# Seven partial products in two more pairs of the first layer, and the sums that they need made beside attention's last units

## Chip, cores and metric

One core of a Trainium2 chip runs the whole kernel. The metric is the device time of one execution in microseconds (us), as the median of several executions. TensorE (PE) multiplies; VectorE (DVE), ScalarE (ACT) and GpSimd (POOL) do the element work; SyncE (SP) issues the loads.

## What is computed

Clustered attention, then two feed-forward layers, all in float32:

```python
mask = q_assign[:, :, :, None] == k_assign[:, :, None, :]
scores = np.where(mask, scale * q @ k.T, -1e9)     # 2 x 8 heads, 768 x 768, head_dim 64
x = softmax(scores) @ v                            # as 1536 tokens x 512
h = x @ w_in;  x = np.maximum(0.01 * h, h) @ w_out # layer one: 512 -> 2048 -> 512
h = x @ w_in2; out = np.maximum(h, 0) ** 2 @ w_out2
```

The assignments are the nearest of 16 centroids, for queries and keys apart; `scale` is 1/8.

## The kernel before

**Precision.** Every float32 operand is kept as two parts, high and low (`xh`/`xl`, `wh`/`wl`, `gh`/`gl`, `th`/`tl`), and every product is three matmuls: high by high, high by low, low by high. A high part is a rounding copy, mostly on ACT; a low part is a subtraction, on POOL or DVE.

**Attention.** 48 units of 256 query rows are taken through scores (`S`), softmax (`e`), transposes (`T`), the split of the transposed weights (`eh`, `el`) and the product with v (`A`). ACT copies one half of `A` out and DVE adds the other (`fold_a`, `fold_b`, into `xt`). When a pair of heads is complete, `xsplit` makes its 128 columns of `xh` and `xl`. The eighth pair of heads holds the last 128 columns for the second 768 tokens.

**The layers.** Tokens are three blocks of 512 (0, 1, 2). The 2048 hidden columns are 16 blocks of 128, taken two at a time: a *pair*, named by its first block (f = 0, 2, ... 14). A weight block is loaded by SP as raw 8-byte words into the one buffer `wraw` (1 MB); ACT (`mag`), POOL (`low`) and DVE (`join`) make float32 words `wt` of it, and only then may the next load start; ACT makes `wh` and POOL `wl`. These steps are the pieces 1 to 4 of `decode_pieces`.

**Plain and seven.** In a plain pair the token blocks are multiplied one by one (`g1`: hidden units `h`; `g2`: outputs `o`). In a pair of the list `SEVEN`, tokens 0 and 1 and the two halves of a weight form 2 x 2 blocks, and seven products take the place of eight, in the first step (`P1` to `P7`) and the second (`M1` to `M7`). This needs sums of weight blocks (`sum_pieces`: four quarter-size operations on POOL into `ws`, then `wh` on ACT and `wl` on POOL) and sums of x: `t1` to `t4`, for both 128-column parts kk = 0 and 1 of each half, each made of whole blocks (`w11`, `w12`, `w21`, `w22`: high plus low, on DVE) by subtraction, and then split into `th` (ACT) and `tl`. `P1`'s result is copied out (`k1`, on ACT) before `P6` is added to the same PSUM bank.

Before, layer one has pairs f = 0 and 2 plain. Pair f = 4 has a plain first step and a seven-product second step (`SEVEN_PLAIN`). The pairs f = 6 to 14 use seven products in both steps.

**Order.** Each engine runs its own instructions in program order and waits on semaphores. From the end of attention to pair f = 2 a scheduler merges the recorded pieces; elsewhere (`manual_schedule`) the engines keep the written order: `PLAN`, `RAMP` and the `SEVEN_...` strings, where each word is one step (`n` the next pair's weights, `u` token block 2, `B` and `T` activations and their sums, `r`, `f`, `o` the flushes).

Of the kernel before, what the change touches and what calls it, by code (L numbers as in the profile page):

```python
# [15 lines left out]
ALU = mybir.AluOpType  # L16
# [47 lines left out]
)  # L64
SEVEN_REST = (
# [34 lines left out]
def attention_moe_moe_kernel(  # L100
# [178 lines left out]

    vp = ast.enter_context(tc.tile_pool(name="vp", bufs=2))  # L280
# [3 lines left out]
    xtp = ast.enter_context(tc.tile_pool(name="xtp", bufs=2))  # L284
# [269 lines left out]
    T_t = {}  # L554

# [58 lines left out]
    def fold_b(u):  # L614
        p, j = divmod(u // UPH, 2)
        c = (u % UPH) * 256
        x = xt_t[p][64 * j : 64 * j + 64, c : c + 256]
        et_t.pop(u)
        nc.vector.tensor_tensor(out=x, in0=a_t.pop(u)[64 * j : 64 * j + 64], in1=x, op=ALU.add)  # L619

    def xsplit(p, part):
        b, hp = divmod(p, HP)
        sl = slice(b * S, (b + 1) * S)
        if part == 0:
            pool_copy(out=xh[:, hp, sl], in_=xt_t[p])
        else:
            nc.gpsimd.tensor_tensor(
                out=xl[:, hp, sl], in0=xt_t.pop(p), in1=xh[:, hp, sl].bitcast(F32), op=ALU.subtract
            )
# [249 lines left out]
    for u in range(-1, NU + 5):  # L879
        if u == NU - UPP:  # L880
            pst.close()
            stg.append(ctx.enter_context(tc.tile_pool(name="stg", bufs=1, side="right", reuse_waits="tile")))
            wpx = ctx.enter_context(tc.tile_pool(name="wpx", bufs=SIDE, side="right", reuse_waits="tile"))
            ring.append((wpx, SIDE))
        if u == NU - 2:
            manual.close()
        for op in PLAN[u % UPP].split():
            if ":" in op:
                name, lag = op.split(":")
                i = u - int(lag)  # L890
# [20 lines left out]
    gp = ctx.enter_context(tc.tile_pool(name="gp", bufs=6, reuse_waits="tile"))  # L911
# [38 lines left out]
    def g1(m, b, f):  # L950
# [5 lines left out]
        return h  # L956

# [96 lines left out]
    def seven(m, f, prev, after, later):  # L1054
# [35 lines left out]
        for name, n, b, block in (  # L1090
            ("g00", "V", 0, f0), ("g01", "U", 0, f1), ("g10", "W", 1, f0), ("g11", "X", 1, f1)
        ):
            ops[name] = lambda n=n, b=b, block=block: prod(
                n, [w_in(block, k) for k in ks], [x_in(k, b) for k in ks], True
            )
# [51 lines left out]
        def unit(j):  # L1147
            st[f"u{j}"] = bank(1 + j * m)
# [108 lines left out]
        for kk in range(2):  # L1257
# [4 lines left out]
            (0, 4): SEVEN_PLAIN, (0, NF - 2): SEVEN_LAST, (1, 2): SEVEN_SEAM, (1, NF - 2): SEVEN_END  # L1262
# [4 lines left out]
    def t_ops(m, kk):  # L1267

        st = {}

        def whole(out, k, b):
            if m:
                st[out] = acc[:, b, k]
                return
            h, l = x_in(k, b)
            st[out] = tmp()
            nc.vector.tensor_tensor(
                out=st[out], in0=h.bitcast(F32), in1=l.bitcast(F32), op=ALU.add
            )

        def minus(out, x, y, *tag):
            st[out] = tmp(*tag)
            nc.gpsimd.tensor_tensor(out=st[out], in0=st[x], in1=st[y], op=ALU.subtract)

        def high(i, t):
            nc.scalar.copy(out=th[:, i, kk], in_=st[t])

        def low(i, t):
            nc.gpsimd.tensor_tensor(
                out=tl[:, i, kk], in0=st[t], in1=th[:, i, kk].bitcast(F32), op=ALU.subtract  # L1290
            )

        def t4():
            minus("t4", "b21", "t2", "t4", 2)
            t_late[kk] = st["t4"]

        def t1():
            if m:
                whole("b12", kk, 1)
                whole("b11", kk, 0)  # L1300
                whole("b22", 2 + kk, 1)
                whole("b21", 2 + kk, 0)
            minus("t1", "b12", "b11")

        return {
            "w12": lambda: whole("b12", kk, 1),
            "w11": lambda: whole("b11", kk, 0),
            "w22": lambda: whole("b22", 2 + kk, 1),
            "w21": lambda: whole("b21", 2 + kk, 0),
            "t1": t1,  # L1310
            "t2": lambda: minus("t2", "b22", "t1"),
            "t3": lambda: minus("t3", "b22", "b12"),
            "t4": t4,
            "h1": lambda: high(0, "t1"),
            "h2": lambda: high(1, "t2"),
            "h3": lambda: high(2, "t3"),
            "l1": lambda: low(0, "t1"),
            "l2": lambda: low(1, "t2"),
            "l3": lambda: low(2, "t3"),
            "h4": lambda: t_last(kk),  # L1320
        }

    def t_last(kk):
        h, l = x_in(kk, 1)
        t = t_late.pop(kk)
        nc.scalar.copy(out=h, in_=t)
        nc.vector.tensor_tensor(out=l, in0=t, in1=h.bitcast(F32), op=ALU.subtract)

    t_late = {}

    def step_list(m, f, prev):
# [28 lines left out]
        else:  # L1360
# [5 lines left out]
        ((0, 1),), ((0, 2),), ((1, 0),), ((0, 3),), ((0, 4), (1, 1)),  # L1366
        ((1, 2),), ((2, 0),), ((1, 3), (1, 4), (3, 0)), ((2, 1),), ((2, 2),),
# [31 lines left out]
    t_by = [[t_ops(m, kk) for kk in range(2)] for m in range(2)]  # L1399

    def sums(m, turn):
        for op in SUMS[m].get(turn, "").split():
            name, kk = op.split(".")
            t_by[m][int(kk)][name]()

    prev = []
    for m in range(2):
        turn = 0
        for f in range(0, NF, 2):
            if (m, f) == (0, 2):  # L1410
                order.enter_context(
                    tc.manual_schedule(
                        engines={
                            mybir.EngineType.PE,
                            mybir.EngineType.DVE,
                            mybir.EngineType.Activation,
                            mybir.EngineType.Pool,
                        }
                    )
                )  # L1420
# [71 lines left out]
```

## Time and profile before

| | |
|---|---|
| median of 3 runs | 738.1 us (737.52 to 738.11) |
| the profiled execution | 737.28 us |
| its span, first to last instruction | 735.6 us |
| PE busy | 729.3 us (99%) |
| POOL / DVE / ACT busy | 580.0 / 555.2 / 491.3 us |
| chain that ended last, share on PE | 94% |
| granted TensorE clock | 1.0 of full speed in every slice |

The span is cut by the profile into busy and idle time for each engine; 1.7 us of the execution's 737.28 lie outside it. Attention ends near 250 us, layer one near 485, layer two at the end.

### The profile page before, as it was taken

To read this page: it belongs to the slowest core of one execution; us is meant where nothing else is said; L and a number is where in the kernel's file an instruction comes from. 1 tells how busy PE (TensorE), PEld (TensorE's weight loads), DVE (VectorE), ACT (ScalarE), POOL (GpSimd) and SP (SyncE) were. 2 spreads that over 40 slices of the span, in tenths; PEclk is the share of its full clock that TensorE was granted. 3 is DMA by queue.
4 is the path that set the end of the run, shared out by engine and by line. 5 is a ranking of instruction groups with operands and counts; after the bars stand their busy time and mean duration, and the time that the engine had idled before them with its cause. 6 is when DMAs were issued, how large, how long until landed. Compare 5 with 4: busy or idle time off the path is not lost.

```text
span 735.6 us, 11900 instructions
## 1 busy us (share of the span) xinstructions
PE 729.3 (99%) x4264; PEld 647.3 (88%) x4264; DVE 555.2 (75%) x879; ACT 491.3 (67%) x909; POOL 580.0 (79%) x534
## 2 busy tenths in 40 slices
PE   9999999999999999999999999999999999999998
PEld 8999999999998888888888888888888898888987
DVE  7999999999998535476766867787676685866847
ACT  7988988988998464456364473657748457484561
POOL 7999999999957648766787877899798786777841
PEclk9999999999999999999999999999999999999999
DMA  5694574572602311111131121211113112121004
GB/s 150 168 224 111 108 186 111 113 180 68 160 22 95 121 70 60 57 58 57 59 115 57 58 91 54 85 57 58 58 58 115 57 58 61 60 110 57 1 1 172
DMA packets 17755, 65.57 MB, mean 89 GB/s; under 512 B 3120, under 2 KB 6320, under 8 KB 12704
## 3 DMA queue, kind: packets, MB, share of 16 engines
q1 hardware_dynamic: 17696, 64.81, 30.0%
q8 instruction: 34, 0.56, 0.3%
q14 instruction: 25, 0.20, 0.1%
HBM read 43.02 MB, written 3.15 MB: 63 GB/s over the span
## 4 chain that ended last, share of the span: by engine, by line
PE 94%; ACT 2%; DVE 2%; POOL 1%; issue 1%; POOLq 0%; ACTq 0%; DVEq 0%
PE h L933 33%; PE o L1170 17%; PE h L1170 10%; PE A L597 8%; PE S L500 8%; PE T L562 7%; PE o L1011 7%; PE S L370 1%; ACT e L532 1%; DVE nm L522 1%; PE warm L310 1%; DVE el L579 1%; ACT eh L573 0%; PE dots L370 0%; POOL e L549 0%
## 5 line engine op out<-in xcount | busy, mean ns | idle before, releaser
L933 PE MATMUL h<-xl,wh 128*128 128x512 f32 x288 | 112.3, 390 | 0.0
L933 PE MATMUL h<-xh,wl 128*128 128x512 f32 x288 | 112.2, 390 | 0.0
L933 PE MATMUL h<-xh,wh 128*128 128x512 f32 x288 | 112.2, 391 | 0.0
L1124 POOL TENSOR_TENSOR gl<-t,gh 128x512 fp32r<-128x512 f32 x52 | 73.1, 1426 | 36.4 <-ACT gh L1121 26.5
L579 DVE TENSOR_TENSOR el<-T,eh 128x512 fp32r<-128x512 f32 x144 | 94.6, 683 | 2.9 <-ACT eh L573 2.2
L549 POOL TENSOR_SCALAR e<-e,r 128x768 f32<-128x768 f32 x96 | 86.3, 908 | 12.7 <-PE T L562 6.8
L532 ACT ACTIVATE e<-S,nm 128x768 f32<-128x768 f32 x96 | 87.3, 909 | 9.8 <-DVE ds L398 5.3
L522 DVE TENSOR_REDUCE nm<-S 128x1 f32<-128x768 f32 x96 | 90.9, 948 | 3.6 <-PE S L370 1.9
L187 POOL TENSOR_TENSOR wl<-ws,wh 128x1024 fp32r<-128x1024 f32 x25 | 60.5, 2419 | 41.8 <-ACT wh L186 41.8
L500 PE MATMUL S<-hb 128*128 128x384 f32 (+1 forms) x384 | 89.5, 347 | 0.1
L187 POOL TENSOR_TENSOR wl<-wt,wh 128x1024 fp32r<-128x1024 f32 x31 | 76.0, 2451 | 12.9 <-ACT wh L186 12.2
L573 ACT CAST eh<-T 128x512 fp32r<-128x512 f32 x144 | 79.7, 590 | 8.8 <-PE T L562 8.6
L597 PE MATMUL A<-eh,vv 128*128 128x256 f32 x288 | 80.3, 308 | 0.6 <-DVE xt L619 0.6
L562 PE MATMUL T<-ident,e 128*128 128x128 f32 x576 | 79.7, 273 | 0.5 <-POOL e L549 0.5
L597 PE MATMUL A<-el,vv 128*128 128x256 f32 x288 | 73.0, 283 | 0.2 <-DVE el L579 0.2
L562 PEld LDWEIGHTS T<-ident,e 128*128 128x128 f32 x576 | 68.9, 143 | 3.6 <-POOL e L549 0.7
L212 ACT ACTIVATE wt<-wraw 128x1024 f32<-128x1024 f32 (+1 forms) x33 | 36.7, 1111 | 49.6 <-POOL ws L267 46.3
L1063 DVE TENSOR_TENSOR h<-h,q 128x512 f32<-128x512 f32 x36 | 25.2, 699 | 54.2 <-PE h L933 48.6
L933 PEld LDWEIGHTS h<-xh,wh 128*128 128x128 f32 x288 | 54.1, 188 | 12.0 <-DVE gl L1124 0.9
L933 PEld LDWEIGHTS h<-xh,wl 128*128 128x128 f32 x288 | 54.0, 188 | 11.3
L500 PEld LDWEIGHTS S<-hb 128*128 128x128 f32 (+1 forms) x384 | 62.2, 189 | 1.6 <-ACT e L532 1.4
L933 PEld LDWEIGHTS h<-xl,wh 128*128 128x128 f32 x288 | 54.1, 188 | 10.6
(190 smaller groups left out, 2051.0 us busy)
## 6 DMA issues: line engine op xcount, KB each, us to landing
wraw<-w SPq DMA_DIRECT2D x32, 1024.0 KB, 4.7
hb<-spl SPq DMA_DIRECT2D x14, 576.0 KB, 4.7
hb<-spl SPq DMA_DIRECT2D x42, 192.0 KB, 5.1
rqk<-qk SPq DMA_DIRECT2D x16, 384.0 KB, 3.7
rv<-v SPq DMA_DIRECT2D x8, 384.0 KB, 3.3
out<-q SPq DMA_DIRECT2D x11, 256.0 KB, 2.2
hb<-st SPq DMA_DIRECT2D x56, 24.0 KB, 1.9
hb<-hb SPq DMA_DIRECT2D x5, 144.0 KB, 8.1
```

The lines of the kernel that those rows point to most:

```text
L187: return lambda eng=nc.gpsimd: eng.tensor_tensor(out=wl, in0=t, in1=wh.bitcast(F32), op=ALU.subtract)
L500: nc.tensor.matmul(out=s[:, c, 0:HALF], lhsT=hb[0:k, a, i * 128 : (i + 1) * 128], rhs=hb[0:k, b, c * HALF : (c + 1) * HALF], start=(a == 0 ...
L522: nc.vector.tensor_reduce(out=n, in_=s_t[t][:, :, 0:HALF], axis=AX.XY, op=ALU.max, negate=True)
L532: nc.scalar.activation(out=e.rearrange("p (a b) -> p a b", a=2), in_=s_t.pop(t)[:, :, 0:HALF], func=AF.Exp, bias=n_t.pop(t), scale=1.0, ac ...
L549: nc.gpsimd.tensor_scalar(out=e_t[t], in0=e_t[t], scalar1=r_t[t // 2][:, t % 2 : t % 2 + 1], scalar2=1.0, op0=ALU.mult, op1=ALU.mult,)
L562: nc.tensor.transpose(T[:, o : o + 128], e_t[2 * u + b][:, kc * 128 : (kc + 1) * 128], ident)
L573: nc.scalar.copy(out=eh[:, 2 * g : 2 * g + 2, :].rearrange("p a b -> p (a b)"), in_=T_t[u, g])
L579: nc.vector.tensor_tensor(out=el[:, 2 * g : 2 * g + 2, :].rearrange("p a b -> p (a b)"), in0=T_t.pop((u, g)), in1=eh[:, 2 * g : 2 * g + 2, ...
L597: nc.tensor.matmul(out=A, lhsT=w, rhs=m[:, kc, :], start=(kc == 0 and i == 0), stop=(kc == KC - 1 and i == 1),)
L933: nc.tensor.matmul(out=out, lhsT=l, rhs=r, start=(first and i == 0), stop=(i == n - 1), skip_group_check=not first,)
L1124: eng.tensor_tensor(out=lo[n], in0=full[n], in1=hi[n].bitcast(F32), op=ALU.subtract)
L1170: nc.tensor.matmul(out=out, lhsT=l, rhs=r, start=(fresh and i == 0), stop=(stop and i == 2), skip_group_check=True,)
```

## The change

- Pairs f = 2 and f = 4 of layer one now use seven products in both steps; f = 2 follows a new order, `SEVEN_TOP`. Three more weight-sum blocks are made.
- The sums of x no longer have two plain pairs in which to be made. Part of them is recorded beside attention's units 46 and 47 (`EARLY_SUMS`), the rest in pair f = 0. They are subtracted in place. Four of the `tl` go from POOL to DVE.
- The last part of `xh` and `xl` is made on ACT and DVE and no longer on POOL.
- Pair f = 0 takes a new order of steps (`first_steps`): the products that don't need the last 128 columns of x run first, the rest follows. From step 6 on, DVE, ACT and POOL keep the written order.

```diff
+SEVEN_TOP = (
+    "P1 k1 P2 aV B11h B11f bh0 P6 k6 P5 k5 B11l n0.1 bh1 P7 aX B22h B22f P3 aW n0.2 "
...
+EARLY_SUMS = ((46, "w12.0 w11.0 w12.1 w11.1 t1.0 t1.1"), (47, "w22.0 t3.0 t2.0"))
...
-    PLAIN = (3, 1)
+    PLAIN = (1, 1)
-    SEVEN = tuple((0, f) for f in range(4, NF, 2)) + tuple((1, f) for f in range(2, NF, 2))
+    SEVEN = tuple((0, f) for f in range(2, NF, 2)) + tuple((1, f) for f in range(2, NF, 2))
+    MANUAL = 6
+    BEHIND = {5: "fold", 6: "xh xl"}
...
+        last = p == NP - 1
         if part == 0:
-            pool_copy(out=xh[:, hp, sl], in_=xt_t[p])
+            if last:
+                low_of["xh"] = nc.scalar.copy(out=xh[:, hp, sl], in_=xt_t[p]).ins
+            else:
+                pool_copy(out=xh[:, hp, sl], in_=xt_t[p])
         else:
-            nc.gpsimd.tensor_tensor(
+            low_of["xl"] = (nc.vector if last else nc.gpsimd).tensor_tensor(
...
+        place = {"t1": "b11", "t2": "b22", "t3": "b12", "t4": "b21"}
+
+        def minus(out, x, y, *tag, eng=nc.gpsimd):
+            st[out] = tmp(*tag) if m else st[place[out]]
...
+            "l1D": lambda: low(0, "t1", nc.vector),
+            "l2D": lambda: low(1, "t2", nc.vector),
...
+    for u, ops in EARLY_SUMS:
+        with tc.issue_after(low_of[u]):
+            for op in ops.split():
+                name, kk = op.split(".")
+                t_by[0][int(kk)][name]()
...
+    def first_steps():
+        held = {}
+        def begin(b, j):
+            held[b, j] = bank((2 * b + j) % 4)
+            g1_part(b, j, held[b, j], range(4 - b))
+        def end(b, j):
+            g1_part(b, j, held[b, j], range(4 - b, 4))
+            act(0, b, j, held[b, j])
+        def ends():
+            end(1, 0)
+            end(1, 1)
+        def unit(b, j):
+            act(0, b, j, g1(0, b, j))
+        return [
+            lambda: unit(0, 0), lambda: begin(1, 0), lambda: begin(2, 0), lambda: unit(0, 1),
+            lambda: begin(1, 1), lambda: g2(0, 0, 0), lambda: g2(0, 0, 1), ends,
+            lambda: end(2, 0), lambda: g2(0, 1, 0), lambda: unit(2, 1), lambda: g2(0, 1, 1),
+        ], [(0, 2, 0), (0, 2, 1)]
...
+            6: "w22.1 h1.0 h2.0 h3.0 h1.1 n2.0 t3.1 t2.1 l1D.0 l2D.0 n2.1 l0.0 w21.0 n2.2 t4.0",
+            7: "h2.1 w21.1", 8: "t4.1 h3.1 l3.0 l3.1", 9: "l1D.1 l2D.1 n3.0",
+            11: "n3.1 h4.0 h4.1 n3.2 n1.4",
```

**DVE at attention's end.** The rows are the last splits of the transposes (`el`), the folds (`xt`), the sums of x (`q`), the `join` of weight block (0, 2, 0) and that of (0, 2, 1) (`wt`). Before:

```order
L579 TENSOR_TENSOR el<-T,eh 128x512
L225 SCALAR_TENSOR_TENSOR wt<-wt,wraw 128x1024
L579 TENSOR_TENSOR el<-T,eh 128x512 x2
L619 TENSOR_TENSOR xt<-A,xt 64x256
L579 TENSOR_TENSOR el<-T,eh 128x512
L982 TENSOR_TENSOR gl<-h,gh 128x512
L1277 TENSOR_TENSOR q<-xh,xl 128x512 x2
L619 TENSOR_TENSOR xt<-A,xt 64x256
```

Now:

```order
L585 TENSOR_TENSOR el<-T,eh 128x512
L934 TENSOR_TENSOR q<-xh,xl 128x512 x4
L230 SCALAR_TENSOR_TENSOR wt<-wt,wraw 128x1024
L585 TENSOR_TENSOR el<-T,eh 128x512 x2
L625 TENSOR_TENSOR xt<-A,xt 64x256
L585 TENSOR_TENSOR el<-T,eh 128x512
L934 TENSOR_TENSOR q<-xh,xl 128x512
L1076 TENSOR_TENSOR gl<-h,gh 128x512
L625 TENSOR_TENSOR xt<-A,xt 64x256
L230 SCALAR_TENSOR_TENSOR wt<-wt,wraw 128x1024
L639 TENSOR_TENSOR xl<-xt,xh 128x768
```

Four sums stand ahead of the `join` that frees `wraw`, and the last `xl` stands behind the next `join`.

**ACT behind the last unit.** `xt` is the last fold's copy, `wt<-wraw` the `mag` of block (0, 2, 1), `acc<-o` the flush of token block 0, `gh` and `h` the activation of token block 1. Before:

```order
L610 COPY xt<-A 64x256
L212 ACTIVATE wt<-wraw 128x1024
L186 CAST wh<-wt 128x1024
L1027 COPY acc<-o 128x512 x4
L976 ACTIVATE gh<-h 128x512
```

Now:

```order
L217 ACTIVATE wt<-wraw 128x1024
L616 COPY xt<-A 64x256
L635 CAST xh<-xt 128x768
L945 CAST th<-q 128x512 x4
L191 CAST wh<-wt 128x1024
L1121 COPY acc<-o 128x512 x3
L191 CAST wh<-ws 128x1024
L1121 COPY acc<-o 128x512
L1070 ACTIVATE gh<-h 128x512
L1071 ACTIVATE h<-h 128x512
```

The `mag` has moved ahead of the last fold's copy, and six casts stand ahead of the activation. Further on in ACT's new order the copy `k1` (`q<-h`) stands behind the `wh` of the second weight sum:

```order
L1121 COPY acc<-o 128x512 x4
L191 CAST wh<-ws 128x1024
L990 CAST xh<-t_3947 128x512
L990 CAST xh<-t_3968 128x512
L1169 COPY q<-h 128x512
```

Before, this pair had no `k1`.

**POOL in pair f = 0.** From the first quarter of the first weight sum to the last of the second (`ws`) POOL now runs the second list (`t_...` are `t4`, `q<-q` other x sums, `tl` their low parts). Before, the same stretch of the program began with the last part of x:

```order
L1283 TENSOR_TENSOR q<-q 128x512
L275 TENSOR_SCALAR xh<-xt 128x768
L1283 TENSOR_TENSOR q<-q 128x512
L627 TENSOR_TENSOR xl<-xt,xh 128x768
L187 TENSOR_TENSOR wl<-wt,wh 128x1024
L219 TENSOR_SCALAR wraw<-wraw 128x1024
L1289 TENSOR_TENSOR tl<-q,th 128x512
L1283 TENSOR_TENSOR q<-q 128x512
```

Now:

```order
L272 TENSOR_TENSOR ws<-wt,ws 128x256
L942 TENSOR_TENSOR q<-q 128x512 x2
L192 TENSOR_TENSOR wl<-ws,wh 128x1024
L942 TENSOR_TENSOR t_3947<-t_3947,q 128x512
L942 TENSOR_TENSOR t_3968<-t_3968,q 128x512
L948 TENSOR_TENSOR tl<-q,th 128x512 x2
L272 TENSOR_TENSOR ws<-wt 128x256
L272 TENSOR_TENSOR ws<-ws,wt 128x256
```

The last part of x has left POOL, and the second weight sum stands behind all of the x sums.

## Rows read from the trace of the kernel before

**Rows 1.** The page's engines: busy us, share of the span, instructions.

```profile
PE 729.3 (99%) x4264; PEld 647.3 (88%) x4264; DVE 555.2 (75%) x879; ACT 491.3 (67%) x909; POOL 580.0 (79%) x534
```

**Rows 2.** Windows: stretch, length, busy us (instructions) of PE, PEld, DVE, ACT, POOL.

```profile
231.00:257.44 26.44, 26.44 (x149) 22.91 (x147) 15.29 (x20) 14.56 (x24) 16.99 (x12) 1.00 0.37 136
257.44:309.19 51.75, 51.75 (x229) 42.73 (x229) 22.89 (x29) 28.67 (x49) 35.15 (x25) 1.00 0.19 67
...
335.03:365.01 29.98, 29.98 (x134) 24.71 (x133) 22.44 (x34) 15.75 (x24) 23.95 (x18) 1.00 0.21 72
```

**Rows 3.** The chain that ended last, one piece: start, us, what.

```profile
265.67 2.72 PE h L933 x12
```

**Rows 4.** Timeline of PE: start, us, line, operation [idle before].

```profile
249.77 0.40 PE L1011 MATMUL o<-gh,wh 128*128 128x512 f32 x1
```

**Rows 5.** Timeline of DVE, 238 to 284 us.

```profile
238.53 0.69 DVE L579 TENSOR_TENSOR el<-T,eh 128x512 fp32r<-128x512 f32 x1 [0.18 <-ACT eh L573]
...
241.96 1.23 DVE L225 SCALAR_TENSOR_TENSOR wt<-wt,wraw 128x1024 int32<-128x1024 int32 x1 [2.73 <-POOL wraw L219]
...
248.22 2.07 DVE L1277 TENSOR_TENSOR q<-xh,xl 128x512 f32<-128x512 f32 x2
250.37 0.43 DVE L619 TENSOR_TENSOR xt<-A,xt 64x256 f32<-64x256 f32 x1
...
252.21 1.84 DVE L225 SCALAR_TENSOR_TENSOR wt<-wt,wraw 128x1024 int32<-128x1024 int32 x1
260.12 0.69 DVE L982 TENSOR_TENSOR gl<-h,gh 128x512 fp32r<-128x512 f32 x1 [6.07 <-ACT h L977]
...
271.81 1.77 DVE L1277 TENSOR_TENSOR q<-xh,xl 128x512 f32<-128x512 f32 x1
...
283.22 2.38 DVE L1277 TENSOR_TENSOR q<-xh,xl 128x512 f32<-128x512 f32 x2
```

**Rows 6.** Timeline of ACT, 240 to 272 us.

```profile
240.70 1.17 ACT L212 ACTIVATE wt<-wraw 128x1024 f32<-128x1024 f32 x1 [2.20 <-DMA wraw<-w]
...
249.97 0.36 ACT L610 COPY xt<-A 64x256 f32<-64x256 f32 x1 [2.39 <-PE A L597]
...
254.08 1.05 ACT L186 CAST wh<-wt 128x1024 fp32r<-128x1024 f32 x1 [2.58 <-DVE wt L225]
257.04 2.06 ACT L1027 COPY acc<-o 128x512 f32<-128x512 f32 x4 [1.90 <-POOL xl L627]
258.95 0.64 ACT L976 ACTIVATE gh<-h 128x512 fp32r<-128x512 f32 x1
...
270.45 1.15 ACT L1286 CAST th<-q 128x512 fp32r<-128x512 f32 x2
```

**Rows 7.** Timeline of POOL, 248 to 294 us.

```profile
248.03 1.12 POOL L219 TENSOR_SCALAR wraw<-wraw 128x1024 int32<-128x1024 uint32 x1 [1.28 <-DMA wraw<-w]
...
252.95 2.25 POOL L1283 TENSOR_TENSOR q<-q 128x512 f32<-128x512 f32 x1
...
256.96 2.40 POOL L187 TENSOR_TENSOR wl<-wt,wh 128x1024 fp32r<-128x1024 f32 x1
...
271.16 1.87 POOL L1289 TENSOR_TENSOR tl<-q,th 128x512 fp32r<-128x512 f32 x1 [10.61 <-ACT th L1286]
272.99 1.74 POOL L1283 TENSOR_TENSOR q<-q 128x512 f32<-128x512 f32 x1
274.70 1.28 POOL L1289 TENSOR_TENSOR tl<-q,th 128x512 fp32r<-128x512 f32 x1
...
282.13 2.32 POOL L1289 TENSOR_TENSOR tl<-q,th 128x512 fp32r<-128x512 f32 x1
...
286.94 2.85 POOL L187 TENSOR_TENSOR wl<-wt,wh 128x1024 fp32r<-128x1024 f32 x1
...
292.52 1.18 POOL L267 TENSOR_TENSOR ws<-wt 128x256 f32<-128x256 f32 x1
293.67 0.73 POOL L267 TENSOR_TENSOR ws<-wt,ws 128x256 f32<-128x256 f32 x1
```

More of the change, by code (lines that the diff above doesn't have):

```diff
@@ L554, in attention_moe_moe_kernel @@
     T_t = {}
+    low_of = {}
     def trans(u, g):
@@ L583, in elo @@
             op=ALU.subtract,
-        )
+        ).ins
     def av(u, lo, hi):
@@ L618, in fold_b @@
         et_t.pop(u)
-        nc.vector.tensor_tensor(out=x, in0=a_t.pop(u)[64 * j : 64 * j + 64], in1=x, op=ALU.add)
+        low_of["fold"] = nc.vector.tensor_tensor(
+            out=x, in0=a_t.pop(u)[64 * j : 64 * j + 64], in1=x, op=ALU.add
+        ).ins
     def xsplit(p, part):
@@ L905, in attention_moe_moe_kernel, with t_last @@
+    def t_last(kk):
+        h, l = x_in(kk, 1)
+        t = t_late.pop(kk)
+        nc.scalar.copy(out=h, in_=t)
+        nc.vector.tensor_tensor(out=l, in0=t, in1=h.bitcast(F32), op=ALU.subtract)
+    t_late = {}
+    t_by = [[t_ops(m, kk) for kk in range(2)] for m in range(2)]
     xsplit(NP - 1, 0)
     xsplit(NP - 1, 1)
+    for u, ops in EARLY_SUMS:
[3 more added lines that the diff above has]
+                t_by[0][int(kk)][name]()
@@ L956, in g1, with g1_part @@
         return h
+    def g1_part(b, f, h, ks):
+        product(h, [w_in((0, 0, f), k) for k in ks], [x_in(k, b) for k in ks], ks[0] == 0)
     parts = {}
@@ L1089, in seven @@
             )
[L1090 to L1095, printed above, removed]
         for name, n in (("k1", "U"), ("k6", "U"), ("k5", "W")):
@@ L1147, in unit @@
         def unit(j):
-            st[f"u{j}"] = bank(1 + j * m)
+            st[f"u{j}"] = bank(1 + j * (m or f == 2))
             product(
@@ L1265, in seven @@
             ops[name]()
[L1267 to L1329, printed above, removed]
+    def first_steps():
[16 more added lines that the diff above has]
+        ], [(0, 2, 0), (0, 2, 1)]
@@ L1397, in pair_after, with sums @@
         return (m, f + 2) if f + 2 < NF else (m + 1, 0)
-    t_by = [[t_ops(m, kk) for kk in range(2)] for m in range(2)]
-    def sums(m, turn):
+    def sums(m, turn, after, later):
         for op in SUMS[m].get(turn, "").split():
             name, kk = op.split(".")
-            t_by[m][int(kk)][name]()
+            if name in t_by[m][0]:
+                t_by[m][int(kk)][name]()
+            else:
+                piece((*(after if name[0] == "n" else later), int(name[1])), int(kk))
     prev = []
     for m in range(2):
-        turn = 0
         for f in range(0, NF, 2):
[L1410 to L1420, printed above, removed]
             after = pair_after(m, f)
@@ L1426, in attention_moe_moe_kernel @@
                 continue
-            seq, prev = step_list(m, f, prev)
+            seq, prev = step_list(m, f, prev) if m else first_steps()
             for i, step in enumerate(seq):
+                if (m, i) == (0, 1):
+                    order.enter_context(tc.manual_schedule(engines={mybir.EngineType.PE}))
                 step()
```

111 lines of the change are left out of this document (84 added, 27 removed), and 7 rows, old and new, of tables (SEVEN_TOP, SUMS).

## The prediction

> **What bounds the kernel now.** I read the page's engine shares first: PE is busy for 729.3 of 735.6 us [rows 1]. Then windows around the change: from 231 us to the end of a full seven-product pair, PE's busy time equals the length of every stretch, while POOL, the next, has 23.95 of 29.98 us in such a pair [rows 2]. So in both layers nothing but PE's own matmuls sets the time, and there are two ways to change it: fewer matmuls, or a new wait in front of one. The chain gives the price of one: twelve matmuls of 512 columns pass in 2.72 us, 0.227 each [rows 3]. (The 0.40 us of a single row [rows 4] is latency; the rows overlap.)
>
> **What is removed.** In pair f = 2 the first step had 4 products x 4 parts x 3 = 48 matmuls and now has 7 x 2 x 3 = 42; its second step goes from 48 to 42 too; so does the first step of pair f = 4. That is 18 matmuls, 18 x 0.227 = 4.1 us. All of it lies on the path, as PE has no idle time here to swallow it.
>
> **What is added off PE, and what hides it.** Per engine the two pairs become like the pair of [rows 2], in which POOL is idle for 6 us, DVE for 7 and ACT for 14. So from f = 4 on I cost the added sums, copies and subtractions at nothing. Without that cover three weight sums would be 16 us of POOL (each four times 0.73 and 2.40, rounded [rows 7]). The loads keep their number and order on SP. The place without cover is pair f = 0, where most of the x sums must now be made, beside attention's end. There I walk each engine's new order with the durations of the rows, first with PE never waiting.
>
> **PE's clock.** Three fewer h matmuls stand ahead of the last attention product, so the first output product, at 249.8 before [rows 4], comes at 249.1. Counting on at 0.227 a matmul, PE wants: its fourth output bank, which attention's last `A` still holds, at 251.1 (nine on); the last `xl` at 254.8 (after 24 outputs and one matmul); `gl` of token block 1 at 257.5 (12 more); the bank of `P1`, emptied by the copy `k1`, for `P6` at 270.9 (96 after the start).
>
> **DVE and the load.** The last common row ends at 239.2 [rows 5]. Four x sums now follow ahead of the `join`. Nearest rows: 0.69 for one operation of that size fed from PSUM, and 1.19 each for two sums that met POOL [rows 5]. POOL is busy for about half of the time; I take 0.9, so the join starts at 242.8 in place of 241.96 and, between its rows of 1.23 and 1.84, ends at 244.2 (before: 243.2). It frees `wraw`. The next load took from 243.2 to POOL's start at 248.0 [rows 7], 4.85 us, so it now lands at 249.05. ACT's `mag` (1.1 [rows 6]) waits for it, and behind it on ACT wait the last fold's copy, `xh` and all that follows. Fold copy 250.5, DVE's fold add 251.0 (0.36 and 0.43 [rows 5, 6]): in time for the fourth bank by 0.1 us, with no margin.
>
> **ACT up to the activation.** `xh` has no row; between a cast of 512 columns (0.6) and one of 1024 (1.05) I take 0.8: 251.8. POOL's `t2`, behind `t3` (to 249.5), the load, its `wraw` step (1.1) and itself 1.3, is ready at 252.0. Then in order: three more `th` (0.53 each), `wh` (1.0), three flushes (0.5 each), `wh` of the weight sum (1.0; POOL has it at 256), a flush (0.5), `gh` and `h` (1.1): 259.0 [rows 6]; DVE's `gl` 0.69 [rows 5]: 259.7. Wanted at 257.5, this is **2.2 us late**. The last `xl` is not: it follows the next join, which ends near 252.3, with 1.5 us or less for 768 columns.
>
> **POOL up to the second weight sum.** It starts the first weight sum when that join ends, 252.3. To the end of the second lie eight quarter operations (0.73), six of 512 columns (1.27) and one `wl` (2.40) [rows 7]: 15.8 us. Meanwhile DVE has eight operations with both inputs in SBUF. What such a meeting costs POOL: rows of 2.25, 1.87, 1.74 and 2.32 stand where 1.28 is the undisturbed time, 2.85 against 2.40, 1.18 against 0.73 [rows 7], together 4.0 us. Eleven such DVE operations met POOL between 248 and 294, eight sums and three joins (of them the rows at 248.22 to 283.22 [rows 5]): 0.36 each. Eight make 2.9: POOL ends at 271.0. ACT's `wh` (1.05), two `xh` (1.05) and `k1` (0.6) follow: 273.7, wanted at 270.9: **2.8 us late**. Both lates are counted from the same clock, so the larger one is the cost, not their sum. Below nothing it can't go: PE has no stall here now that it could give back. At its ends: if meetings cost POOL nothing, `k1` is in time and ACT's 2.2 decide; if each cost 0.52 (282.13, two operations, 1.03 [rows 7]), it is 4.1.
>
> The Trainium skill (SBUF — State Buffer, "SBUF: two separate sides") says that DVE with two SBUF inputs and GpSimd share a port under an exclusive lock, the loser blocked for the whole instruction. By it each of the eight would cost POOL its whole length. The trace agrees only in part, with 0.36 us of about 0.65; what full blocking would make here is the second rival.
>
> After `P6` I find no further wait: `P7` needs `t3`'s low parts at 276.5 and POOL has them at 268; the second weight sum's `wl` (274.5) is first needed by `M6` after 288.
>
> **Sum.** Against the profiled execution's own time: 737.28 - 4.1 + 2.8 = 736.0 us. The median shown lies 0.8 above that execution; carried over, 736.8. I give **736.7**.
>
> **Rivals.** (1) *The waits are smaller.* For it: each link of the walk has 0.1 to 0.4 of rounding, and POOL took a `wraw` step beside two DVE sums at no cost (1.12 [rows 7]). ACT's queue alone gives 2.2, and 1.0 if the load is early and the fold goes straight after PE: 734.2 to 735.4 own. Against: 7.2 us of ACT work still lie between `xh` and `gl`, and PE leaves 5.7.
>
> (2) *DVE and POOL exclude each other fully.* Then eight operations cost POOL 5.5 us (seven of 0.65, the row's 0.69 less the overlap of rows, and 0.95 for 768 columns) and not 2.9; `k1` comes 5.4 after PE wants it: 738.6 own, +0.18%, still within the bound below. For it: at 283.22 two sums and one POOL operation took nearly the sum of their times [rows 5, 7]. Against: the other rows show half of that.
>
> (3) *The late load: slower.* Each us by which the join of block (0, 2, 0) slips moves the load, `mag`, the last fold, the fourth bank, `xh` and the next join, and so both lates, by the same us; from a slip of 2.8 us beyond my 244.2 (a join that ends after 247) the sum passes 738.7 own, slower. This needs 1.6 per sum and not 0.9, for which no row but the single longest, 1.77 for one sum, speaks: the four would each have to meet POOL at its worst, and POOL idles for part of that time.
>
> (4) *The change does what its count says and nothing waits*: 733.2 own. All of ACT's six casts would have to fit before 252; I see no cover.
>
> **Chances.** Forecast (waits of 2.2 to 3.4) 0.49; rival 1 0.25; rival 2 0.09; rival 3 0.09; rival 4 0.08. A measurement of this kernel tells 0.2%, 1.5 us, from no change; the forecast's 1.3 to 1.4 lies on that edge, so 0.15 of its 0.49 (waits under 2.6) count as faster. Faster: 0.15 + 0.25 + 0.08 = 0.48; same 0.34 + 0.09 = 0.43; slower 0.09. The range leaves out rivals 2 and 3, together 0.18: from no wait (733.2 own, 734.0 as a median) to one of 4.5 us (738.5), which covers the bounds of the meetings, 2.2 and 4.1.
>
> **What would show it.** In the profile after: PE idle in front of the first output product of token block 1, released by DVE's `gl`, about 2 us, and in front of `P6`, released by ACT's `q` copy, the remaining 0.6, or all at one of them; no PE idle from pair f = 4 on, and pairs of 30.0 us. DVE's four sums from 239.2, 3 to 4 us long; the last fold's copy released by a load or by `mag`, not by PE; POOL busy without a gap from 252 to 271. Wrong would be: PE without idle time there (rival 4), a wait for the fourth bank above 1 us (rival 3), or waits in pair f = 2 behind `P6`, which I cost at nothing.

## The result, and the profile after

The changed kernel takes **742.2 us** (median of 6 runs, 741.5 to 742.9) against 737.6 (737.3 to 738.1) for the kernel before: ratio 1.0061, 95% interval 1.0048 to 1.0074. It is slower, where 736.7 and no loss were forecast. Its profiled execution took 741.67 us, 4.4 above that of before.

The page's engines, as in [rows 1], with the clock line of the slices:

```profile
span 739.9 us, 11917 instructions
...
PE 728.2 (98%) x4246; PEld 645.3 (87%) x4246; DVE 575.0 (78%) x899; ACT 499.0 (67%) x922; POOL 598.3 (81%) x547
...
PEclk9999999999999989999999999999999999999999
```

The 18 matmuls are gone (4264 to 4246), and the span is still 4.3 us longer. One slice of the clock line, at about 265 us, is not full. The waits of PE, largest first (us in total, times, longest), show three new ones, all in pair f = 0:

```profile
PE o L1105 <- ACT gh L1070: 2.9, 1, 2.9
...
PE o L1105 <- DVE xt L625: 1.0, 1, 1.0
...
PE o L1105 <- DVE gl L1076: 0.4, 1, 0.4
```

Those left out stood there before. The timeline of PE at the new waits, a matmul behind them, and the first of `P6` (the last row):

```profile
251.78 0.50 PE L1105 MATMUL o<-gh,wh 128*128 128x512 f32 x1 [0.97 <-DVE xt L625]
...
261.10 0.80 PE L1105 MATMUL o<-gh,wh 128*128 128x512 f32 x1 [2.91 <-ACT gh L1070]
262.31 0.79 PE L1105 MATMUL o<-gl,wh 128*128 128x512 f32 x1 [0.42 <-DVE gl L1076]
...
278.27 0.39 PE L1027 MATMUL h<-th,wh 128*128 128x512 f32 x1
```

Windows (stretch, length, busy us of PE, PEld, DVE, ACT, POOL, then the granted clock):

```profile
258.00:261.00 3.00, 0.19 (x1) 0.00 (x0) 1.54 (x2) 2.22 (x5) 2.92 (x3) 0.95 0.00 0
261.00:267.00 6.00, 5.48 (x12) 4.01 (x13) 5.12 (x6) 3.58 (x8) 6.00 (x4) 0.50 0.00 0
...
268.00:274.00 6.00, 6.00 (x28) 4.92 (x27) 0.96 (x2) 3.60 (x7) 5.50 (x6) 1.00 0.01 3
```

PE had next to nothing from 258 to 261; then its granted clock was 0.50, the lower of its two levels (1.2 GHz), and 12 matmuls passed in six us where 28 pass later. The chain that ended last runs through the engines ahead of that wait (start, us, what; its pieces of "issue" between these, each under 0.1 us, are left out):

```profile
241.54 2.31 DVE q L934 x2
243.85 1.15 DVE wt L230
245.01 4.71 DMA wraw<-w
249.75 1.13 ACT wt L217
250.90 0.37 ACT xt L616
251.30 0.44 DVE xt L625
251.78 2.35 PE o L1105 x9
254.13 1.44 POOL ws L272
255.64 3.36 POOL ws L272 x3
259.02 1.04 ACT wh L191
```

It reads: two of the four x sums, the join behind them, the load, `mag`, the fold, the fourth bank; then the first weight sum on POOL, and its cast `wh`, which stands on ACT ahead of the activation that PE waits for. ACT and POOL there [rows 6, 7]:

```profile
254.17 1.67 ACT L945 CAST th<-q 128x512 fp32r<-128x512 f32 x3 [1.06 <-POOL q L942]
255.75 1.04 ACT L191 CAST wh<-wt 128x1024 fp32r<-128x1024 f32 x1
256.70 1.54 ACT L1121 COPY acc<-o 128x512 f32<-128x512 f32 x3
259.02 1.04 ACT L191 CAST wh<-ws 128x1024 fp32r<-128x1024 f32 x1 [0.78 <-POOL ws L272]
259.97 0.58 ACT L1121 COPY acc<-o 128x512 f32<-128x512 f32 x1
260.45 0.60 ACT L1070 ACTIVATE gh<-h 128x512 fp32r<-128x512 f32 x1
```
```profile
251.81 2.33 POOL L942 TENSOR_TENSOR q<-q 128x512 f32<-128x512 f32 x1
254.11 1.45 POOL L272 TENSOR_TENSOR ws<-wt 128x256 f32<-128x256 f32 x1
255.64 1.07 POOL L272 TENSOR_TENSOR ws<-ws,wt 128x256 f32<-128x256 f32 x1
256.67 1.19 POOL L272 TENSOR_TENSOR ws<-wt 128x256 f32<-128x256 f32 x1
257.82 1.17 POOL L272 TENSOR_TENSOR ws<-wt,ws 128x256 f32<-128x256 f32 x1
```

The quarters take 4.9 us; undisturbed they are 0.73 each, 2.9 [rows 7].

**The account.** The first output product came at 248.58, 1.2 earlier than in [rows 4]: 0.7 for three of the removed matmuls, 0.5 that the execution's attention was ahead. From there 96 matmuls at 0.227 would put `P6` at 270.4; it came at 278.27, **7.9 late**: 1.0 + 2.9 + 0.4 of waits, and 3.6 for the lower clock and the restarts. Behind `P6` PE waits for nothing. Behind PE's last matmul lie 4.54 us to the end of the span, where the kernel before had 3.35: **1.2 more**. Sum: -4.1 - 0.5 + 7.9 + 1.2 = +4.5, measured +4.4.

### The profile page after: what moved, and what is told of

It is laid out like the page before. It is cut to its first block, busy times and chain, and to the rows that moved or that the text cites. A ratio compares the mean times of both kernels' runs of the same rounds, so it can differ in the third digit from the quotient of the medians.

```text
span 739.9 us, 11917 instructions
## 1 busy us (share of the span) xinstructions
PE 728.2 (98%) x4246; PEld 645.3 (87%) x4246; DVE 575.0 (78%) x899; ACT 499.0 (67%) x922; POOL 598.3 (81%) x547
## 4 chain that ended last, share of the span: by engine, by line
PE 84%; ACT 4%; POOL 4%; DVE 4%; DMA 2%; issue 1%; ACTq 0%; POOLq 0%; DVEq 0%
PE h L1027 30%; PE o L1258 16%; PE h L1258 9%; PE A L603 8%; PE S L505 8%; PE T L568 7%; PE o L1105 4%; PE S L375 1%; DMA wraw<-w 1%; ACT e L537 1%; POOL ws L272 1%; DVE nm L527 1%; POOL wl L192 1%; POOL e L554 1%; PE warm L315 1%
## 5 line engine op out<-in xcount | busy, mean ns | idle before, releaser
L1212 POOL TENSOR_TENSOR gl<-t,gh 128x512 fp32r<-128x512 f32 x56 | 80.1, 1448 | 34.3 <-ACT gh L1209 21.8
L1027 PE MATMUL h<-xh,wh 128*128 128x512 f32 x272 | 106.6, 392 | 0.0
L1027 PE MATMUL h<-xh,wl 128*128 128x512 f32 x272 | 106.2, 390 | 0.0
L1027 PE MATMUL h<-xl,wh 128*128 128x512 f32 x272 | 106.1, 390 | 0.0
L192 POOL TENSOR_TENSOR wl<-ws,wh 128x1024 fp32r<-128x1024 f32 x28 | 67.9, 2425 | 41.6 <-ACT wh L191 41.6
L1157 DVE TENSOR_TENSOR h<-h,q 128x512 f32<-128x512 f32 x42 | 29.3, 699 | 64.1 <-PE h L1027 54.6
L1212 DVE TENSOR_TENSOR gl<-h,gh 128x512 fp32r<-128x512 f32 x70 | 47.9, 687 | 18.5 <-ACT h L1194 7.9
L1027 PEld LDWEIGHTS h<-xh,wh 128*128 128x128 f32 x272 | 51.3, 188 | 11.3 <-DVE gl L1212 1.1
L1027 PEld LDWEIGHTS h<-xh,wl 128*128 128x128 f32 x272 | 51.1, 188 | 10.7
```

What stands on the lines that cost most here:

```text
L192: return lambda eng=nc.gpsimd: eng.tensor_tensor(out=wl, in0=t, in1=wh.bitcast(F32), op=ALU.subtract)
L1027: nc.tensor.matmul(out=out, lhsT=l, rhs=r, start=(first and i == 0), stop=(i == n - 1), skip_group_check=not first,)
L1212: eng.tensor_tensor(out=lo[n], in0=full[n], in1=hi[n].bitcast(F32), op=ALU.subtract)
```

## The experiments

Medians in us; ratios against the kernel before, run on the same chip, with the 95% interval in brackets.

**Which wait, and what is behind it.** Two moves, each alone and both together. e1 moves the weight sum's cast alone; e2 moves all that stands ahead of the activations (the lists are issued behind steps 6 and 7):

```diff
-6: "w22.1 h1.0 h2.0 h3.0 h1.1 n2.0 t3.1 t2.1 l1D.0 l2D.0 n2.1 l0.0 w21.0 n2.2 t4.0", 7: "h2.1 w21.1",
+6: "w22.1 h1.0 h2.0 h3.0 h1.1 n2.0 t3.1 t2.1 l1D.0 l2D.0 l0.0 w21.0",                      (e1)
+7: "n2.1 n2.2 t4.0 h2.1 w21.1",
+6: "w22.1 n2.0 t3.1 t2.1 l0.0 w21.0",                                                       (e2)
+7: "h1.0 h2.0 h3.0 h1.1 n2.1 l1D.0 l2D.0 n2.2 t4.0 h2.1 w21.1",
```

e3 puts `k1` ahead of the second weight sum's cast; e4 is e2 and e3:

```diff
-11: "n3.1 h4.0 h4.1 n3.2 n1.4",
+11: "n1.4",
-"P1 k1 P2 aV B11h B11f bh0 P6 k6 P5 k5 B11l
+"P1 k1 P2 aV B11h B11f bh0 P6 k6 P5 k5 h4.0 h4.1 c3.1 c3.2 B11l
```

> Edit: ACT's cast of the weight sum (wh from ws) goes behind the two activations of token block 1; nothing else moves on any engine but the order of that cast. Theory A (two lates in a row: first ACT's queue in front of gh and gl, behind it and hidden by it the copy k1 that waits for POOL's second weight sum): gh starts straight behind the fourth flush, about 258.7 in place of 260.45; PE's wait for gh falls from 2.9 to about 1.1, gl adds up to 1; k1 still comes near 276, so P6 moves forward by 2 us at most: 740.2 to 741.5. Rival B (no second late; all 7.9 us come from the one wait and the half clock behind it): 738 to 739 if the clock then stays at 1.00. Rival C (POOL's slow quarters of the weight sum are not what ACT waits for; the four casts th are): gh no earlier than 260, time unchanged within 0.5.

Measured: 741.5, 1.0058 (1.0044 to 1.0072). Waits of 1.1 for `gh` and 0.7 for `gl`, the clock lower for about half as long, and a new wait of 1.3 in two pieces for ACT's `q` copies: theory A, at the top of its range. The ratio itself is not clear of the changed kernel's (1.0048 to 1.0074); the waits tell the theories apart.

> Edit: on ACT the flushes and both activations of token block 1 go ahead of four casts th and of the weight sum's cast; on DVE their gl go ahead of two low parts tl. Theory A: no wait of PE for gh or gl is left, PE's granted clock stays at 1.00 (in the changed kernel it was 0.50 from 260.85 to 267.7), P6 would be wanted at 278.3 - 2.9 - 0.4 - 2.4 - 0.5 = 272.1; k1 stands on ACT behind the second weight sum's cast, which came at 276.2 and now by perhaps one us earlier, so a new wait of 3 to 4 us opens in front of P6, released by ACT's q copy: 739.2 to 740.2. Rival B (no second late): 736.0. Rival C (the load and the last fold are late, not ACT's order): a wait of over 1.5 us for gh stays and the time is above 741.

Measured: 742.8, 1.0074 (1.0061 to 1.0087). The largest wait of PE now:

```profile
PE h L1027 <- ACT q L1169: 3.9, 1, 3.9
```

The wait for `gh` is gone (0.5 for `gl` stays), and in its place PE stands 3.9 us in front of `P6`, for `k1`. ACT and PE show from where, and what follows:

```profile
274.78 1.04 ACT L191 CAST wh<-ws 128x1024 fp32r<-128x1024 f32 x1 [6.05 <-POOL ws L272]
...
276.77 0.58 ACT L1169 COPY q<-h 128x512 f32<-128x512 f32 x1
```
```profile
277.40 0.80 PE L1027 MATMUL h<-th,wh 128*128 128x512 f32 x1 [3.86 <-ACT q L1169]
...
278.42 0.63 PE L1027 MATMUL h<-th,wl 128*128 128x512 f32 x1
278.85 0.63 PE L1027 MATMUL h<-th,wh 128*128 128x512 f32 x1
```

Matmuls of 0.63 at a pitch of 0.43: the clock fell here too (mean 0.76 over 272 to 280, 0.79 over 280 to 287). Theory A had the wait right and its price wrong, because it left the clock out: the second late cost as much as the first.

> Edit: the copy k1, the sum aV and pair f=2's first activation go ahead of the second weight sum's cast and of the casts of t4. Theory A: alone it is worth nothing, since P6 did not wait in the changed kernel (k1 ended at 276.2, P6 started at 278.27): 742.2 within 0.5, PE's waits for gh (2.9) and the half clock unchanged. A theory in which the second weight sum sets the time through k1 expects 2 us or more less: 740.

Measured: 743.4, 1.0083 (1.0069 to 1.0096). No gain, as theory A said, but 743.4 is outside its 0.5: PE has new waits of 0.3 for ACT's `q` at 311.8 and of 1.0 for DVE's `gl` at 445.2, far behind the edit, in pair f = 12 by the pairs' 30 us. POOL stood idle for 7.9 until the late cast; that this idle time leads to the wait at 445 is not shown.

> Edit: both of the two moves before. Theory A: neither wait is left but about 1.0 us for the fourth output bank; clock at 1.00; 742.2 - 2.9 - 0.4 - 2.4 - 0.5 = 736.0 (735.3 to 736.7), below the kernel before (737.6) by about 1.5. Rival B: the same as the run with the activations ahead alone. Rival C: above 741. If the two lates were independent costs and not one behind the other, the gains of the two single runs would add up to this one's; theory A expects them to sum to about 2.5 and this one to 6.

Measured: 737.7, 1.0000 (0.9990 to 1.0009). 4.6 us better than the changed kernel, where the two moves alone lost 0.6 and 1.1: one late stood behind the other. It missed 736.0 by the waits of 1.0 for `gl`, again far on, and 0.2 for ACT, with what PE loses restarting behind each, and PE's first output product stood 0.8 later in this execution (249.39):

```profile
439.12 0.50 PE L1027 MATMUL h<-xh,wh 128*128 128x512 f32 x1 [0.95 <-DVE gl L1212]
```

The clock stayed at 1.00 over 250 to 300.

**The clock's own price.** e7 is e3 with twelve matmuls into a bank that nobody reads:

```diff
+        def fill():
+            spare = bank(1)
+            wh, _ = weights[0, 0, 0]
+            for _ in range(12):
+                nc.tensor.matmul(out=spare, lhsT=wh[:, 0:128], rhs=xh[:, 0, 0:N], start=True, stop=True)
-            lambda: end(2, 0), lambda: g2(0, 1, 0), ...
+            lambda: (end(2, 0), fill()), lambda: g2(0, 1, 0), ...
```

> Edit against the run with k1 ahead alone (743.4): PE issues twelve more matmuls of 512 columns (2.7 us) into a spare bank just ahead of the product that waits 2.9 us for gh; nothing reads them. They add no time as long as they fit into the wait. Theory (the 0.50 clock that followed PE's idle time costs by itself): the granted clock stays at 1.00, the products behind pass at 0.227 and not 0.427, 740.7 (740.3 to 741.2). Rival (the slow pitch is a matter of the weights, of PE's queue or of the operands, not of the clock and the idle time): the pitch stays, 743.4 or slightly more.

Measured: 740.7, 1.0048 (1.0030 to 1.0066), 2.7 below e3. Its timeline and windows:

```profile
258.84 2.88 PE L1375 MATMUL h<-xh,wh 128*128 128x512 f32 x12
261.88 0.51 PE L1105 MATMUL o<-gh,wh 128*128 128x512 f32 x1 [0.15 <-ACT gh L1070]
263.09 0.51 PE L1105 MATMUL o<-gl,wh 128*128 128x512 f32 x1 [0.71 <-DVE gl L1076]
263.44 0.40 PE L1105 MATMUL o<-gh,wl 128*128 128x512 f32 x1
```
```profile
262.00:268.00 6.00, 5.29 (x23) 4.12 (x23) 5.34 (x6) 3.37 (x7) 6.00 (x4) 1.00 0.01 3
```

Needless work in a wait that stays as long made the kernel faster: the clock is 1.00 in this execution and in five others. In two of the eight (743.8 and 744.3) the mean granted clock was 0.995 and nothing was gained, so the filling does not hold the clock every time. Nor do executions alone price it: e3's four lie within 0.1 us at mean clocks of 0.995 to 0.998. PE's last matmul came 2.0 earlier than in e3, which is the clock's; the other 0.8 belong to the end, which was also shorter here (last group).

**The late load and the fold.** e8 makes ACT copy the last fold ahead of `mag` (`low_of["copy"]` is that copy):

```diff
-    BEHIND = {5: "fold", 6: "xh xl"}
+    BEHIND = {4: "copy", 5: "fold", 6: "xh xl"}
```

> Edit against the changed kernel (742.2): ACT copies the last fold ahead of mag, alone. Theory (waits one behind the other, all counted from the same clock; what sets gh is POOL's weight sum and the join ahead of it, which this leaves where they are): the wait of 1.0 for the fourth bank goes and the wait for gh grows by about as much; 742.2 within 0.5. Rival (the waits are independent and add up): 741.0.

Measured: 741.5, 1.0046 (1.0029 to 1.0062). The bank's wait went and was handed on: 0.7 for `xl`, 2.8 for `gh`, 0.7 for `gl`, 0.5 for ACT. 0.2 below the expected range, with the clock lower for a shorter time (mean 0.72 over 262 to 268); the ratio is not clear of the changed kernel's. e5 is e4 with the second cast straight behind `k6`, which feeds POOL; e6 is e5 with the edit of e8; e10 is e6 with the last `xl` ahead of the join (`5: "xl"` in place of `5: "fold"`):

```diff
-bh0 P6 k6 P5 k5 h4.0 h4.1 c3.1 c3.2 B11l
+bh0 P6 k6 c3.1 c3.2 P5 k5 h4.0 h4.1 B11l
```

> Edit against the run with both moves (737.7): the second weight sum's cast goes straight behind the copy k6 and ahead of the casts of t4, so that POOL, which stood idle for 1.35 us in front of its wl, has it in time. Theory: the two small waits of PE that were left later (1.0 for DVE's gl near 299, 0.2 for ACT's copy near 305) come down the queue from that idle time; they go: 736.5 (736.1 to 737.0). Rival (they come from the loads or from DVE): 737.7, waits unchanged.

Measured: 737.4, 0.9993 (0.9984 to 1.0003). The two waits went (the first had stood at 439.1, not near 299; why a move in pair f = 2 opens or ends a wait so far on is not shown); one of 1.3 for DVE's `h` came, as DVE's sum for `P3`'s bank now stood behind the low parts of `t4`.

> Edit against the run before (e5_pool_fed): ACT copies the last fold ahead of the activation mag that waits for the load. Theory: the fold itself is done when PE's last attention product is, at about 250; the wait of 1.0 for the fourth output bank is the load's, handed on by ACT's order; it goes, with its restart of 0.25, and no other takes its place as gh, gl and k1 are early by about 1: 1.2 less than e5_pool_fed, 735.3 (734.8 to 736.0), 2 below the kernel before. Rival (xl or the load's join are next in line at once): less than 0.4 better, with a new wait of PE for DVE's xl.

Measured: **736.5**, 0.9978 (0.9969 to 0.9988): faster than both kernels. PE's waits in the changed part are down to

```profile
PE h L1027 <- DVE xl L639: 0.7, 1, 0.7
...
PE h L1027 <- DVE h L1157: 0.2, 1, 0.2
```

so 0.9 of the 1.2 against e5 came, and the rival had the next in line right, though not its 0.4.

> Edit against e6_fold_first (736.5): DVE makes the last xl ahead of the join of the second load. Theory: PE's wait of 0.7 for xl and its restart go, POOL's two weight sums come 1.0 later, which the slack now ahead of their users takes up but for 0.2: 735.7 (735.3 to 736.3). Rival (no slack: the later weight sums hand the time back through the copies k5 and k6): 736.5 or more, with a new wait of PE for DVE's h or ACT's q behind 275.

Measured: 737.4, 1.0001 (0.9992 to 1.0010). The rival, though at another place: the later join pushed its cast `wh` in front of two flushes and `gh` (waits of 0.5 and 0.7), and DVE's `h` came 0.9 late.

**What a meeting of DVE and POOL costs.** e9 adds six sums to e6, where DVE was idle and POOL was not:

```diff
+            for i in range(6):
+                h, l = x_in(i % 4, 0)
+                add(acc[:, 2, i % 4], h.bitcast(F32), l.bitcast(F32))
```

> Edit against the run with the fold ahead (e6_fold_first, 736.5): six more sums on DVE, each 512 columns with both inputs in SBUF, into space that is written again before anyone reads it, at the place where DVE was idle from 270.4 to 276.4 and POOL ran four quarters of the second weight sum (0.74 each, gapless) and a wl (2.41), 5.3 us from 271.24 to 276.56. This prices a meeting of DVE and POOL by itself. Theory of full exclusion (each holds off the other for a whole operation): POOL's stretch lengthens by about 0.65 for each sum that falls into it, 3 to 4 us for six, and the sums take 1.3 or more each in place of 0.65. The forecast's 0.36 for each: 2.2 us. No contention: 0, and six sums in 3.9 us. The time: up to 1 us more, as POOL's later work is handed on.

Measured: 741.9, 1.0064 (1.0050 to 1.0078). DVE and POOL:

```profile
270.31 8.91 DVE L1157 TENSOR_TENSOR acc<-xh,xl 128x512 f32<-128x512 f32 x6
```

```profile
271.23 1.19 POOL L272 TENSOR_TENSOR ws<-wt 128x256 f32<-128x256 f32 x1
272.50 1.07 POOL L272 TENSOR_TENSOR ws<-ws,wt 128x256 f32<-128x256 f32 x1
273.53 1.18 POOL L272 TENSOR_TENSOR ws<-wt 128x256 f32<-128x256 f32 x1
274.67 1.19 POOL L272 TENSOR_TENSOR ws<-wt,ws 128x256 f32<-128x256 f32 x1
275.81 2.86 POOL L192 TENSOR_TENSOR wl<-wt,wh 128x1024 fp32r<-128x1024 f32 x1
```

Each POOL operation lost 0.33 to 0.45 (0.74 and 2.41 alone), 2.1 from 271.23 to the end of `wl`, near the forecast's 0.36. But each DVE sum took 1.49 where one alone takes some 0.65: DVE lost more than POOL, and the forecast had no price for that side. The Trainium skill (SBUF — State Buffer, "SBUF: two separate sides") has the pair of ports held by one engine for a whole instruction, the other blocked; the DVE side agrees (a sum takes 0.84 more, about what a quarter of 0.74 takes), POOL's 0.45 is less than a whole sum. The time missed the 1 us expected: DVE's later sum for a PE bank came 4.0 us late, and PE's clock fell behind that wait (0.62 over 284 to 291).

**The end of the kernel.** Second profiles of both kernels:

> The kernel before, a second profile, for the stretch from PE's last matmul to the end of the span: 3.35 us in its first profile, 4.55 in that of the changed kernel, 3.3 in the run with fill. If that stretch is the change's own, it is 3.3 to 3.4 here again; if it only varies from execution to execution, any value from 3.3 to 4.6 may come.

> The changed kernel once more, on the chip of these runs: 742.2, and a second profile. All PE waits as before it (1.0, 2.9, 0.4) and 6.8 us of clock at 0.50 behind the second, since they hang on the order of instructions alone; the stretch behind PE's last matmul 4.55 if it is the change's own, else anything from 3.3 to 4.6.

Measured: 736.9 (one run) and 741.7, 1.0065 (1.0051 to 1.0079); 3.33 and 4.50 us behind PE's last matmul. So it is each kernel's own. What differs is when one instruction load (queue 8, a whole block of 16 KB) comes. DMA views of before (724 to 728 us) and after (731 to 735 us), issues with KB and median us to landing:

```profile
q8 instruction: 1, 0.02, 1.8%
...
out<-q SPq DMA_DIRECT2D x4, 256.0 KB, 2.4
```
```profile
q8 instruction: 1, 0.02, 2.7%
...
out<-q SPq DMA_DIRECT2D x4, 256.0 KB, 4.0
```

In before the load starts 10.6 us ahead of the end, as the last stores begin; in after 7.6, among them, and these take 4.0 and not 2.4 us to land. Of all profiles:

```
load starts, us ahead of the end     us from PE's last matmul to the end
10.3 to 10.7: before, again, e7      3.35 3.33 3.26
              e11 e12 e13 e14        3.26 3.26 3.27 3.27
6.3 to 7.6:   after, again, e1 e2    4.54 4.50 4.58 4.25
              e3 e4 e5 e6            4.03 4.60 4.10 4.08
              e8 e9 e10              4.11 4.07 4.43
```

18 x 0.227 = 4.1 us is what the change took out of PE's program ahead of that place. Counted to PE's last matmul the load moved by 4.2 (7.25 ahead of it in before, 3.02 in after). It does not go by the count alone: the twelve matmuls of e7 brought it back to 7.05, as far as all eighteen would. The Trainium skill (Runtime: NRT & Kernel Launch, "Instruction fetch mechanics") says that an engine's program is refilled in blocks of 256 instructions at a cost mostly hidden; the 34 such loads in the profile's queue 8 fit the 2 x 4246 instructions of PE and PEld (33.2 blocks), but by the table one among the stores was not hidden. To move it back, e12 splits the changed kernel's first nine warm-up matmuls (two instructions each), e11 does it in e6, and e13 is e11 with POOL's `t2` behind the first weight sum:

```diff
+        c = 64 if n == 9 else 128
-        for i in range(n):
-            nc.tensor.matmul(out=w[:, 0:128], lhsT=ident, rhs=ident, start=True, stop=True)
+        for i in range(n * 128 // c):
+            nc.tensor.matmul(out=w[:, 0:c], lhsT=ident, rhs=ident[:, 0:c], start=True, stop=True)
```

> Edit against the changed kernel (742.2 and 741.7): its first nine warm-up matmuls of 128 columns, before any data is there, become eighteen of 64; each is two instructions of PE, so 18 more stand ahead of everything, as many as the change removed, in the same time. Theory (the changed kernel's PE program is 18 matmuls shorter, so a load of instructions at a fixed place in it comes 18 x 0.227 = 4.1 us nearer to the end, among the last output stores): that load moves back to 11 us ahead of the end, the stretch behind PE's last matmul falls from 4.5 to 3.3, 741.0 (740.6 to 741.4); all waits in the middle as before. Rival (the stretch belongs to the stores or their buffers, not to the instruction load): 742.0, the stretch stays at 4.5 wherever the load is.

> The same edit in the best version so far (e6_fold_first, 736.5, stretch 4.08): by the theory 735.75 (735.3 to 736.2); by the rival 736.5.

> Edit against the run before (e11_warm_more_best): POOL's difference t2 goes behind the first weight sum, so that DVE's join and last xl no longer meet it. Theory (a meeting holds DVE off for most of POOL's operation: xl took 2.06, and 0.96 where it met none): xl about 0.5 earlier or more, PE's wait of 0.6 to 0.7 for it shrinks to 0.2 or none: 735.2 (734.8 to 735.8). Rival (xl meets the first quarter of the weight sum instead and loses as much): as the run before.

Measured: 749.7 (1.0161, 1.0147 to 1.0175), 743.9 (1.0082, 1.0068 to 1.0096) and 743.8 (1.0084, 1.0070 to 1.0098). The times are spoiled at the start: e12's first row of PE

```profile
1.41 7.94 PE L316 MATMUL warm<-ident 128*128 128x64 f32 x36 [1.41 <-POOL ident masks.py:199]
```

shows 0.22 a matmul, no less than for 128 columns (in the changed kernel 18 take 3.83, 0.21 each), and all else came later. PE also stayed at the slow pace far longer: nine matmuls of 128 columns (`ohT`) took 1.97 at 18.1 us and 1.30 at 20.4, where the changed kernel has 1.15 at 10.1. The windows print 1.00 there, but the trace's first record of the granted clock, 1.00, stands at 19.8 us in e12 and at 4.7 in the changed kernel. But the load stands at 10.5 again, and the end is 3.26 in all three: the theory of the load. e13 gave nothing: the wait for `xl` went, others of 0.7 and 0.6 came. e14 puts twelve matmuls of 16 columns into e6's wait for `xl` (as `fill` above, with `spare[:, 0:16]` and `xh[:, 0, 0:16]`, ahead of `ends`):

> Edit against the run with the fold ahead (e6_fold_first, 736.5): twelve matmuls of 16 columns into a spare bank, read by nobody, just ahead of the x products of token block 1, where PE waits 0.7 us for DVE's xl. They need 0.06 to 0.12 each, 0.7 to 1.4 in all, of which 0.7 lies in the wait. Theory (place of the instruction load): it moves from 7.5 to about 10 us ahead of the end, the stretch behind PE's last matmul falls from 4.08 to 3.3: 735.7 to 736.4 by the cost of the twelve. Rival (the stretch only goes with programs that are slow at the start or elsewhere): stretch 4.1 and 736.5 to 737.2.

Measured: 736.6, 0.9984 (0.9975 to 0.9993). End 3.27, as expected; the 0.8 won there went to a wait of 1.3 for DVE's `h` that the shifted order opened, and to the twelve (1.4, half of it in the wait). So no time shows the end's price by itself; the profiles do.

## Why the prediction was wrong

**Right.** The 18 matmuls went at 0.227 each; PE's due times held (first output 248.58 against 249.1 less 0.5); no wait came behind `P6`; the two places of waits, `gl` and `k1`, were the right ones, and both lates are counted from one clock, so that they don't add up (e2, e3, e4).

**Mis-sized: DVE and the load.** Four sums at 0.9 were to take 3.6; they took

```profile
238.59 5.26 DVE L934 TENSOR_TENSOR q<-xh,xl 128x512 f32<-128x512 f32 x4
```

in the changed kernel, 1.3 each, beside two POOL operations. The join ended 0.8 later (1.3 in before's count, with the 0.5 of attention), the load 0.7 (1.2), and the fourth bank, "in time by 0.1 us, with no margin", became a wait of 1.0. The forecast had chosen between 0.69 and 1.19 by POOL's share of busy time; e9 shows 1.49 for a sum that meets POOL each time. The 0.8 carried over from the profiled execution to the median was also too much: 0.3 with six runs (737.6).

**The step that failed: ACT up to the activation.** The forecast said "POOL has it at 256"; POOL had the weight sum at 259.0, 259.5 in before's count. Of these 3.5 us, 1.2 are the load and the join behind it; 1.1 come from `t2`, which took 2.33 for 1.3 beside the join and `xl` and still stood in front of the quarters; 1.2 are the quarters, 4.9 for the 3.7 left to them from the join's end at 252.3. `gl` came 5.3 late where 2.2 were forecast. The meetings had been priced one by one for the second weight sum; for the first, the walk on ACT took a time of POOL's without them.

**Mis-sized: `k1`.** Forecast 2.8 late; in the changed kernel it ended at 276.2, 276.7 in before's count, 5.8 late. Of the 3.0 more, 2.3 are the first weight sum's later start, the load, the join and `t2` again; the stretch from there to the end of the second took 19.5 where 18.7 were forecast, so the price of 0.36 a meeting held for POOL within 0.8. It did not show only because the wait for `gh` and what followed had put `P6` back by 7.9, more than `k1`'s 5.8. e2 uncovered it.

**Not in the sum at all: the clock.** The forecast priced a wait at its length. PE's idle 2.9 us brought half the clock for some six more, 2.0 us (e7). And **the end**: 1.2 us, shown by the loads' places.

**The rivals.** Rival 3 had the sign and the late load, but its point, a join that ends after 247, was not reached (245.0): slower came from sizes that were all off to the same side, and from two terms that nobody had. Rival 1's smaller waits did not come. Rival 2's full blocking is too much for POOL, and rival 4's kernel without waits was not reached by any order tried: the best, e6, is 0.22% faster than before.

**Open.** Why the load among the stores costs 0.7 in one order and 1.3 in another, and what sets its place; no time, only profiles, shows its price by itself. What ties the order in pair f = 2 to the wait near 440 (e3, e4, e7). Why the same wait of 2.9 was followed by 6.8 us of half clock in the changed kernel and by 3.4 in e12.

## What to carry to other kernels

Where a pipeline has no slack, walk every engine's queue with the durations that it has beside its new neighbours, on both sides of the meeting, and give each late its follower: fixing one wait uncovers the next, so look for what is second. Take the place of a wait from the timeline and not from its line: one stood 160 us behind the edit. Price an idle matmul engine above its idle time if the profile shows the clock falling behind it; work that nobody needs can be worth putting there. When a change alters an instruction count, compare the kernel's end too, although no edit touches it.

## What the hardware showed that was not expected

- The granted clock stayed at 1.00 behind single waits of 1.0 to 1.3 us (e4, e5). It fell to 0.50 for 6.8 us behind waits of 2.9 to 4.0 (after, e2, e3, e9), but for 3.4 behind one of 2.8 (e8), one of 2.9 (e12), and waits of 1.1 and 0.7 in a row (e1).
- A DVE sum with both inputs in SBUF took 1.49 beside a busy POOL, and each POOL operation beside such sums lost 0.33 to 0.45 (e9).
- One instruction load of 16 KB among the last stores went with 0.7 to 1.3 us more behind the last matmul (18 profiles).
- The first matmuls took 0.22 of 64 columns (e12) and 0.21 of 128 (after); with those of 64 PE's slow pace lasted to about 20 us, with those of 128 to 5 or 6.
